# A spectral filter and a state-space recurrence on one core: units of 256 tokens by four state blocks, B kept in SBUF, and the inverse transform carried to the output tiles

## The chip, the cores and the metric

The kernel runs on one core of one Trainium2 chip. The metric is device time in microseconds (us), the median of several executions. The engines are called as in the profile: PE is TensorE's matmul, PEld its weight load, DVE is VectorE, ACT is ScalarE, POOL is GpSimd, and SP is SyncE, whose queue (SPq) issues nearly all DMAs here. L12 means line 12 of the kernel that was profiled.

## The reference, cut to what matters

```python
# x: [1, 2048, 1024]; all inputs bf16
g = sigmoid((x * gate_w).sum(-1, keepdims=True))
a = irfft2(rfft2(x) * (w_r + 1j * w_i))            # over tokens and channels
Lam_bar = exp(dt * Lam); B_bar = ((Lam_bar - 1) / Lam)[:, None] * Bmat
Bu = einsum("bld,pd->blp", x, B_bar)               # 1024 complex states
for t in range(2048): h = Lam_bar * h + Bu[:, t]   # kept for every t
b = 2 * einsum("blp,dp->bld", hseq, Cmat).real + x * Dskip
out = g * a + (1 - g) * b
```

The kernel does the two-dimensional FFT as matrix products in stages, with one transposition through DRAM on the way forward and one on the way back. The recurrence is done by rotating into a frame in which the state only shrinks by a real factor: two products by cosine and sine tables, a scan on VectorE, two products back. In both kernels FFT work and recurrence work are interleaved.

## The kernel before: what the change and the argument touch

B is loaded transposed in the first of four token chunks, stored to a DRAM scratch, and loaded again from it in the other three. A recurrence unit is 512 tokens by two state blocks.

```python
TC = 512
def fetch_BT(c, jb):
    BTs = btp.tile([P, 2, 8, P], BF16, name="BTs")               # two buffers
    if c == 0:
        for ri, src in enumerate((B_B_re, B_B_im)):
            nc.sync.dma_start_transpose(out=BTs[:, ri], in_=src[P * jb:P * (jb + 1), :])
        nc.sync.dma_start(out=bt_dram[jb], in_=BTs)
    else:
        nc.sync.dma_start(out=BTs, in_=bt_dram[jb])
    BTq[c, jb] = BTs

def ssm(c, q, u, h):
    sh = [P, 2, 2, TC]
    # two products by the table, add, subtract        ... (cut)
    for j in range(2):
        jb = 2 * q + j
        rb = r_sb[:, jb:jb + 1].to_broadcast([P, TC])
        for ri in range(2):
            nc.vector.tensor_tensor_scan(out=g[:, j, ri, :], data0=rb, data1=v[:, j, ri, :], ...)
    # two products by the table, add, subtract        ... (cut)
```

The two columns of W that need a correction (k = 0 and k = 512) are loaded:

```python
nc.gpsimd.dma_start(out=Wc[:, :, 0], in_=Wr_v[:, :, 0])          # and three more like it
```

The inverse FFT ends with two small products for each of 16 groups of tokens. The first is evicted to ZT; the second consumes it at once, and the result goes to a DRAM scratch that the last stage reads again:

```python
ZT = gt.tile([P, 8, P], BF16, name="ZT", tag="gev")
nc.scalar.copy(out=ZT, in_=psz.rearrange("p kc (c q) -> p (kc c) q", c=2))
...
nc.tensor.matmul(psy[:, cls, :], lhsT=ZT[:, 4 * cls + i, :], rhs=Gi_sb[:, 4 * cls + i, :], ...)
...
nc.sync.dma_start(out=ga_v[:, bp, :], in_=ga.rearrange("p h n -> p (h n)"))
```

The start loads four x tiles, then the first block of B (two transposing loads and the store), then the other x tiles as buffers come free:

```python
for r in range(4):
    load_x(r)
fetch_BT(0, 0)
for r in range(4):
    turn_x(r)
    load_x(r + 4)
```

## Time and profile before

| | before |
|---|---|
| time, median of 4 runs beside the changed kernel | 462.67 us (458.96 to 470.05) |
| span of the profiled run | 464.6 us (that run took 466.38 us, 1.6% above the fastest, so it is marked slow) |
| TensorE busy | 378.8 us |
| VectorE busy | 289.4 us |
| DMA | 67.30 MB |
| first B product | 63.5 us |
| first FFT matmul | 72.3 us |

A run is called slow when it lies more than 1.5% above the fastest run of the same kernel. The only trace of the kernel before is of a slow run, so its stage times are read with that in mind.

The page gives busy time for each engine, then the span in 40 slices of 11.6 us: a digit is the busy share in tenths, PEclk the granted TensorE clock in tenths.

```profile
PE 378.8 (82%) x1958; PEld 185.3 (40%) x1993; DVE 289.4 (62%) x420; ACT 191.8 (41%) x251; POOL 5.9 (1%) x11
...
PE   2005599899999675988895998899998999997996
...
PEclk9999689999999997999998899999999999999799
DMA  8999306464546999878867546431212223310121
```

TensorE is the busiest engine. The holes are the first five slices, the stretch from slice 14 to 20, and single slices later. The table of stretches (length, busy time and instruction count of each engine, clock, DMA share, GB/s) shows the first hole and part of the second:

```profile
0.00:20.00 20.00, 4.00 (x29) 2.89 (x29) 4.01 (x23) 6.22 (x10) 5.87 (x11) 1.00 0.88 144
20.00:40.00 20.00, 2.91 (x19) 2.04 (x20) 2.41 (x13) 2.09 (x3) 0.00 (x0) 1.00 1.19 172
40.00:63.00 23.00, 14.78 (x110) 7.79 (x109) 11.87 (x16) 19.86 (x30) 0.00 (x0) 0.78 0.45 150
...
145.00:180.00 35.00, 23.00 (x131) 9.89 (x132) 31.29 (x57) 11.86 (x15) 0.00 (x0) 0.95 0.99 255
```

In the first 63 us TensorE works 22 us. From 145 to 180 us VectorE (31.29 of 35 us) and the DMA engines (0.99) are nearly full and TensorE is not. The list of waits (waiting engine, line, releaser: total us, times, longest) names what held TensorE:

```profile
PE pt L165 <- DMA xn<-in_A_x_dram: 26.3, 3, 22.3
PE psu L276 <- DMA BTs<-bt_scratch: 14.0, 6, 5.5
```

So x came late at the start, with one wait of 22.3 us, and TensorE waited 14 us for reloads of B.

### The profile page before, as it was taken

To read this page: it belongs to the slowest core of one execution; us is meant where nothing else is said; L and a number is where in the kernel's file an instruction comes from. 1 tells how busy PE (TensorE), PEld (TensorE's weight loads), DVE (VectorE), ACT (ScalarE), POOL (GpSimd) and SP (SyncE) were. 2 spreads that over 40 slices of the span, in tenths; PEclk is the share of its full clock that TensorE was granted. 3 is DMA by queue.
4 is the path that set the end of the run, shared out by engine and by line. 5 is a ranking of instruction groups with operands and counts; after the bars stand their busy time and mean duration, and the time that the engine had idled before them with its cause. 6 is when DMAs were issued, how large, how long until landed. Compare 5 with 4: busy or idle time off the path is not lost.

```text
span 464.6 us, 5250 instructions
## 1 busy us (share of the span) xinstructions
PE 378.8 (82%) x1958; PEld 185.3 (40%) x1993; DVE 289.4 (62%) x420; ACT 191.8 (41%) x251; POOL 5.9 (1%) x11
## 2 busy tenths in 40 slices
PE   2005599899999675988895998899998999997996
PEld 1003235444444231433341555544444444443442
DVE  2012556667868899798993121259995269999212
ACT  0406989899965431366660566640000011110000
POOL 5000000000000000000000000000000000000000
PEclk9999689999999997999998899999999999999799
DMA  8999306464546999878867546431212223310121
GB/s 138 116 134 343 103 9 139 145 194 136 164 153 227 181 289 243 179 245 263 276 216 125 165 161 223 156 117 45 82 56 92 90 92 136 108 62 13 47 89 45
DMA packets 71153, 67.30 MB, mean 145 GB/s; under 512 B 45780, under 2 KB 50260, under 8 KB 70744
## 3 DMA queue, kind: packets, MB, share of 16 engines
q1 hardware_dynamic: 70280, 65.08, 49.9%
q10 hardware_dynamic: 656, 1.88, 2.1%
q0 software_dynamic: 192, 0.02, 0.8%
q8 instruction: 15, 0.25, 0.2%
q14 instruction: 10, 0.08, 0.1%
HBM read 37.57 MB, written 21.00 MB: 126 GB/s over the span
## 4 chain that ended last, share of the span: by engine, by line
PE 36%; DVE 14%; DMA 9%; issue 5%; ACT 4%; SPq 3%; ACTq 0%; DVEq 0%
PE ps_y L547 15%; PE psu L276 11%; DVE g L294 5%; PE ps_id L489 5%; DMA BTs<-bt_scratch 4%; DMA Bb<-turn_scratch 2%; ACT eo L492 2%; DVE o L556 2%; DVE pb L302 2%; PE ps_fd L326 1%; DMA W_b<-in_A_w_r_dram 1%; PE ps_y L551 1%; SPq L653 1%; DMA W_b<-in_A_w_i_dram 1%; DVE pa L301 1%
## 5 line engine op out<-in xcount | busy, mean ns | idle before, releaser
L276 PE MATMUL psu<-xT,BTs 128*128 128x512 bf16 x498 | 121.2, 384 | 15.1 <-DMA BTs<-bt_scratch 14.0
L547 PE MATMUL ps_y<-CT_1199,h 128*128 128x512 bf16 x250 | 96.2, 385 | 5.6 <-DVE o L556 5.1
L547 PE MATMUL ps_y<-CT_1200,h 128*128 128x512 bf16 x250 | 96.2, 385 | 0.3
L276 PEld LDWEIGHTS <-BTs 128*128 128x128 bf16 x512 | 49.5, 99 | 74.2 <-DMA BTs<-bt_scratch 17.7
L547 PEld LDWEIGHTS <-h 128*128 128x128 bf16 x512 | 49.6, 99 | 61.2 <-issue 8.3
L278 ACT CAST u<-psu 128x1024 bf16<-128x1024 f32 x32 | 32.3, 1014 | 84.7 <-PE psu L276 80.1
L294 DVE TENSOR_TENSOR_SCAN g<-r_sb,carry,v 128x512 bf16<-128x512 f32 x48 | 58.4, 1266 | 0.0
L556 DVE SCALAR_TENSOR_TENSOR o<-ps_y,omg,gac 128x1024 bf16<-128x1024 f32 x16 | 20.5, 1279 | 37.4 <-PE ps_y L551 37.4
L165 PE MATMUL pt<-ident,xn 128*128 128x128 bf16 x128 | 11.6, 254 | 31.9 <-DMA xn<-in_A_x_dram 26.3
L494 DVE TENSOR_TENSOR ga<-eo 128x512 bf16<-128x512 bf16 x16 | 6.8, 425 | 47.9 <-ACT eo L492 47.9
L326 PE MATMUL ps_fd<-G_sb,preT 128*128 128x512 bf16 x125 | 29.9, 379 | 3.9 <-ACT X_684 L329 1.0
L489 PE MATMUL ps_id<-Gi_sb,ZT 128*128 128x512 bf16 x126 | 29.9, 378 | 3.1 <-ACT eo L492 3.0
L285 DVE TENSOR_TENSOR v<-u,tab 128x2048 bf16<-128x2048 bf16 x16 | 19.6, 1223 | 16.0 <-ACT u L278 15.8
L492 ACT ACTIVATE eo<-ps_id,gA 128x1024 bf16<-128x1024 f32 x16 | 17.8, 1115 | 17.1 <-issue 14.6
L326 PEld LDWEIGHTS <-preT 128*128 128x128 bf16 x128 | 18.5, 144 | 15.3 <-issue 6.2
L166 ACT COPY xT<-pt 128x1024 bf16<-128x1024 bf16 x16 | 15.3, 1007 | 20.6 <-PE pt L165 20.6
L165 PEld LDWEIGHTS <-xn 128*128 128x128 bf16 x128 | 9.6, 115 | 35.2 <-DMA xn<-in_A_x_dram 28.1
L298 ACT CAST glast<-g 128x4 f32<-128x4 bf16 x12 | 2.4, 199 | 48.1 <-DVE g L294 48.1
L301 DVE TENSOR_TENSOR pa<-g,tab 128x2048 bf16<-128x2048 bf16 x16 | 19.6, 1224 | 0.4
L489 PEld LDWEIGHTS <-ZT 128*128 128x128 bf16 x128 | 12.4, 97 | 18.1 <-issue 5.6
L286 DVE TENSOR_TENSOR su<-u,tab 128x2048 bf16<-128x2048 bf16 x16 | 19.5, 1219 | 0.0
L302 DVE TENSOR_TENSOR pb<-g,tab 128x2048 bf16<-128x2048 bf16 x16 | 19.5, 1218 | 0.0
(553 smaller groups left out, 487.3 us busy)
## 6 DMA issues: line engine op xcount, KB each, us to landing
BTs<-bt_scratch SPq DMA_DIRECT2D x24, 512.0 KB, 4.4
xn<-in_A_x_dram SPq DMA_DIRECT2D x16, 256.0 KB, 3.7
bt_scratch<-BTs SPq DMA_DIRECT2D x8, 512.0 KB, 2.7
Bb<-turn_scratch SPq DMA_DIRECT2D x16, 256.0 KB, 4.1
Cq<-turn_scratch SPq DMA_DIRECT2D x16, 256.0 KB, 2.7
ga_scratch<-ga SPq DMA_DIRECT2D x16, 256.0 KB, 2.4
gac<-ga_scratch SPq DMA_DIRECT2D x16, 256.0 KB, 4.4
out_dram<-o SPq DMA_DIRECT2D x16, 256.0 KB, 2.1
```

The lines of the kernel that those rows point to most:

```text
L165: nc.tensor.transpose(out=pt[:, j8, :], in_=xns[r][:, P * j8:P * (j8 + 1)], identity=ident)
L276: nc.tensor.matmul(psu[:, ri, :], lhsT=BTs[:, ri, d8, :], rhs=xT[:, d8, TC * c:TC * (c + 1)], start=(d8 == 0), stop=(d8 == 7))
L278: nc.scalar.copy(out=u_out, in_=psu)
L285: nc.vector.tensor_mul(out=v, in0=u, in1=tab[:, js, 0:1, :].to_broadcast(sh))
L294: nc.vector.tensor_tensor_scan(out=g[:, j, ri, :], data0=rb, data1=v[:, j, ri, :], initial=(0.0 if c == 0 else carry[:, jb, ri:ri + 1]), o ...
L301: nc.vector.tensor_mul(out=pa, in0=g, in1=tab[:, js, 2:3, :].to_broadcast(sh))
L302: nc.vector.tensor_mul(out=pb, in0=g[:, :, ::-1, :], in1=tab[:, js, 3:4, :].to_broadcast(sh))
L326: nc.tensor.matmul(ps[:, cls, :], lhsT=preT_A[:, cls, d4, j, :], rhs=G_sb[:, cls, d4, :], start=(d4 == 0), stop=(d4 == 3))
L489: nc.tensor.matmul(psy[:, cls, :], lhsT=ZT[:, 4 * cls + i, :], rhs=Gi_sb[:, 4 * cls + i, :], start=(i == 0), stop=(i == 3))
L492: nc.scalar.activation(out=eo, in_=psy, func=ACT.Copy, scale=gA[:, bp:bp + 1])
L547: nc.tensor.matmul(psy[:, 512 * dh:512 * (dh + 1)], lhsT=hs[jb // 2][:, jb % 2, ri, P * tq:P * (tq + 1)], rhs=CT[ri][:, jb, 512 * dh:512 * ...
L556: nc.vector.scalar_tensor_tensor(out=o, in0=psy, scalar=omg[:, tb:tb + 1], in1=gac, op0=ALU.mult, op1=ALU.add)
```

## The change

Its intent: take the B scratch and the FFT result scratch away, run the forward FFT first and without interruption, halve the rotation tables, and do the last product of the inverse FFT beside the output product C of each token tile, so that the FFT result need not be stored in between.

```diff
-TC = 512
+TC = 256
+NEARLY = 4
...
+    BT = [btp.tile([P, 2, 8, P], BF16, name=f"BT{jb}") for jb in range(8)]      # B stays
+    xn = [t.rearrange("p r j m -> p r (j m)") for t in BT]                     # x is loaded there first
+    for i in range(8):
+        nc.sync.dma_start(out=xn[i], in_=x[2 * P * i:2 * P * (i + 1), :].rearrange("(r p) d -> p r d", p=P))
...
+    def unit(c, q):                                  # 256 tokens by four state blocks
+        u = b_unit(c, q)
+        ...  # same products and sums, in place; 8 scans of 256 in place of 4 of 512
...
             A1 = gta.tile([P, 2, K], BF16, name="A1")
-            nc.scalar.copy(out=A1, in_=psa)
-            nc.scalar.copy(out=Acol[:, j, :], in_=psa[:, :, 0])
+            nc.vector.tensor_copy(out=A1, in_=psa)
+            nc.gpsimd.tensor_copy(out=Acol[:, j, :], in_=A1[:, :, 0])
             nc.sync.dma_start(out=turn1_dram[j], in_=A1)
...
-            ZT = gt.tile([P, 8, P], BF16, name="ZT", tag="gev")
-            nc.scalar.copy(out=ZT, in_=psz.rearrange("p kc (c q) -> p (kc c) q", c=2))
+        ZT = fft["ZT"]                               # [P, 8, 16, P]: all 16 groups at once
+        ZT_v = ZT.rearrange("p i q (a b) -> p b i q a", b=16)
+        for bp in range(16):
+            ...
+            nc.scalar.copy(out=ZT_v[:, bp], in_=psz.rearrange("p kc (c q a) -> p (kc c) q a", c=2, a=8))
...
+    def finish(tb, psy=None):                        # for one tile of 128 tokens
+        pse = psU.tile([P, 2, K], FP32, name="ps_id", tag="psu")
+        ...  lhsT=fft["ZT"][:, 4 * cls + i, tb, :], rhs=fft["Gi"][:, 4 * cls + i, :]
+        ...  # scale by g, add and subtract, add (1 - g) times the C product, store to the output
...
-        nc.gpsimd.dma_start(out=Wc[:, :, 0], in_=Wr_v[:, :, 0])
-        ...  # three more
+            for ri, W in enumerate((A_w_r, A_w_i)):
+                fl = W.rearrange("s k -> (s k)")[K:K + (S - 1) * (K + 1)].rearrange("(s k) -> s k", k=K + 1)
+                nc.sync.dma_start(out=Wp[0:P - 1, ri], in_=fl[0:S - 16, 0:2].rearrange("(p b) k -> p b k", b=16))
+                ...  # three small loads for what is left
```

First, the final token order is 128 consecutive tokens to a tile, while group bp of the inverse FFT yields tokens bp, bp + 16, and so on; so the copy to ZT now writes 2-byte elements 32 bytes apart. The last element of one row of W lies next to the first of the following row, so both columns are now loaded as pairs, 4 bytes each.

## The prediction

> **What bounds the kernel now.** By the page, TensorE is busy 379 of 465 us. Its pitches in the timeline (start to start, full clock) are 0.216 us for 512 columns, 0.109 for 256; so all matmuls need 346 us, and about 118 us is lost. The table of stretches and the waits show where:
> - Start, 0 to 63 us: 22 us of TensorE work. The longest wait is 22.3 us for x tiles: in the timeline the DMA queue stands from 7 to 33 us at the store of B, behind two transposing loads; VectorE stands 17.75 us for W columns.
> - 145 to 256 us (forward product, W): TensorE 87 of 111 us, VectorE 96, DMA share 0.76 to 0.99; B reloads waited for 14 us. After a 5.0 us wait at 254.7, 256-column matmuls step 0.213 us for 4 us. The Trainium skill (TensorE: Matmul & The Clock Gate, Part 1) says that an idle window of about 3.4 us halves the clock; this trace agrees.
> - End: from 417 to 432 us VectorE's recurrence holds TensorE up.
>
> **What changes.** Removed: 4 MB of B stores, 12 MB of reloads, 8 MB of FFT result scratch, gate scratch, the column patch (8 us near 245). Halved: table making. Added: 4 MB of float32 scratch, 64 scans. A scan steps 1.18 us for 512 elements; I estimate 0.65 for 256, 5.2 us a unit against 4.7. A unit then costs VectorE 12.9 us (4 products at 1.16, 4 sums at 0.63, scans, carry). A1 (1.15 us, 16 times) and half the x evictions move from ScalarE to VectorE. B's 1024 matmuls of 256 columns take 112 us, as before.
>
> **Timeline of the new order.**
> - Start: x first in the queue; 4 MB at 90 ns per 2048-byte packet on 16 engines, 14 us. VectorE's evictions and sums, 22 us: forward FFT begins near 27.
> - Forward FFT, 16 steps: matmuls 1.9, ScalarE 1.31, two handovers: 3.4 us a step (5.1 before), to 82.
> - Turn through DRAM, filled with B products, 17 us and the fixup: to 100.
> - W stage, 16 steps: VectorE bounds it, 15 x 1.9 plus three units, 67 us; DMA about 3.6 us a step, close behind. To 169.
> - Then TensorE-bound: is2 14, inverse 28, B 62, C 118: 222 us, VectorE 176. ScalarE costs is2 4 to 6 us; gaps and cold clock 8; tail 5.
>
> Sum about 410: 36 us saved at the start, the rest mostly in the middle.
>
> **Prediction: 410 us, range 395 to 428. Chances: faster 0.97, same 0.02, slower 0.01.**
>
> **What would show it.** First FFT matmul at 24 to 32 us; forward steps 3.2 to 3.7 us apart; W stage 62 to 80 us, VectorE over 90% busy; 256-scans near 0.65 us pitch; B matmuls at 0.109; from the first C product on TensorE busy over 93%, no bubble in the last 40 us; DMA bytes near 46 MB.
>
> **What would make it wrong.** The transposing B loads (16 behind x in one queue, each waiting for TensorE to leave its buffer) could arrive late and delay the T3 table and the stores. The six shared h buffers could hold VectorE after the sixth unit (I expect 15 us, off the critical path); if VectorE cannot catch up, the C stage is VectorE-bound, +10 to 20. DMA latency with two buffers in the W stage: +10. In-place products or 256-element rows slower than 1.16: +5.

## The result

| | before | after |
|---|---|---|
| time, median of 4 runs | 462.67 us | 497.5 us (495.55 to 499.25) |
| ratio, 95% interval | 1 | 1.0781 (1.0698 to 1.0863): slower |
| span profiled | 464.6 us | 495.2 us |
| TensorE busy | 378.8 us | 391.8 us |
| VectorE busy | 289.4 us | 314.5 us |
| DMA | 67.30 MB | 46.37 MB |
| first B product | 63.5 us | 27.1 us |
| first FFT matmul | 72.3 us | 29.9 us |

A ratio here compares the fast runs of the two kernels in the same rounds, while the medians are taken over all runs, so it is not quite the ratio of the medians quoted beside it. The spread of the kernel before from run to run (459 to 470 us here) is wider than that of most variants.

The start came out as foreseen: the first B product came 36.4 us earlier. DMA fell by a third; yet the kernel lost 35 us. The page after, same lines (a slice is now 12.4 us):

```profile
PE 391.8 (79%) x2568; PEld 244.5 (49%) x2601; DVE 314.5 (64%) x532; ACT 211.6 (43%) x195; POOL 18.3 (4%) x42
...
PE   4797306989979777554444699999999999999994
...
PEclk9789656999989999965555599999999999999999
DMA  8999012213418998862210202200120130001001
```

There are two new holes. In slices 5 and 6 (3 and 0 tenths) TensorE nearly stops. In slices 18 to 23 it is "busy" about half the time at a granted clock of 5 to 6 tenths. From slice 24 to the end it is full, as predicted. The table of stretches of the kernel after:

```profile
46.00:78.00 32.00, 6.03 (x22) 2.92 (x21) 2.34 (x3) 4.41 (x8) 0.70 (x4) 0.61 0.17 33
...
146.00:212.00 66.00, 49.16 (x307) 29.11 (x311) 61.24 (x112) 36.51 (x52) 9.48 (x16) 0.99 0.89 228
212.00:281.00 69.00, 34.71 (x152) 21.50 (x152) 23.41 (x36) 66.13 (x17) 0.00 (x0) 0.52 0.22 68
...
342.00:444.00 102.00, 101.53 (x689) 66.16 (x697) 99.32 (x149) 22.53 (x22) 0.00 (x0) 1.00 0.14 47
```

The W stage (146 to 212) is bound by VectorE, 61.24 of 66 us, as predicted, and the stage of the C products has no bubble. From 212 to 281 us only ScalarE is full, 66.13 of 69 us, in 17 instructions, and the TensorE clock is 0.52. From 46 to 78 us no engine is busy for more than 6.03 of the 32 us.

**Stretch 212 to 281.** The instructions of the line that copies to ZT (duration min/median/max in ns, first and last start), and the chain that ended last (start, length, what):

```profile
L455 ACT CAST ZT<-ps_is_2045 x1: 4751/4751/4751, 241.5 to 241.5; 128x1024 bf16<-128x1024 f32 x1
L455 ACT CAST ZT<-ps_is_2057 x1: 4747/4747/4747, 245.8 to 245.8; 128x1024 bf16<-128x1024 f32 x1
```

```profile
211.47 4.24 DMA Cq<-turn_scratch
215.77 64.80 ACT ZT L455 x15
```

The copies of 128x1024 elements take 4.75 us each and start 4.3 us apart. A copy of the same shape and types, PSUM to bf16, takes 1.01 us elsewhere in the same trace, as this line of the page shows (busy us, mean ns of one):

```profile
L260 ACT CAST u<-psu 128x1024 bf16<-128x1024 f32 x32 | 32.2, 1012 | 60.9 <-PE psu L258 47.0
```

The same copy to ZT took 1.00 us in the kernel before, where it was contiguous. Fifteen of the slow copies are 64.80 us in a row on the chain. TensorE works about 2 us between two of them and then idles. The Trainium skill (TensorE: Matmul & The Clock Gate, Part 1) puts the half clock down to idle windows of about 3.4 us. This trace agrees only in part: the slow matmuls begin after a wait of 5.5 us (L258, for the eviction u), but the waits for the copies were only 2.0 to 2.8 us, and the mean clock of the stretch was 0.52 all the same. With contiguous copies (first experiment below) it was 0.99 in this stage, from 216 to 232 us.

**Stretch 46 to 78.** The SP queue in order of time (start, length of the issue on the queue, line, destination and source):

```profile
45.98 0.38 SPq L325 DMA_DIRECT2D turn_scratch<-A_602  x1
46.40 0.88 SPq L586 DMA_DIRECT2D Wp<-in_A_w_r_dram  x1
47.33 12.27 SPq L587 DMA_DIRECT2D Wp<-in_A_w_r_dram  x1
...
60.52 0.71 SPq L586 DMA_DIRECT2D Wp<-in_A_w_i_dram  x1
61.34 12.04 SPq L325 DMA_DIRECT2D turn_scratch<-A_622  x1
```

L586 is the load of 127 partitions, once for the real and once for the imaginary part. Its own issue takes 0.7 to 0.9 us; the next issue then stands for 12.27 and 12.04 us. The second time the one that stands is the store of an A1 tile of the forward FFT. TensorE meanwhile waits for VectorE to evict the next A1 tile:

```profile
L318 PE MATMUL ps_s_677<-X_655,T_sb 128*128 128x512 bf16 x1 | 0.6, 586 | 23.6 <-DVE A_662 L323 23.6
```

VectorE is held in two ways by the same queue. A1 has two buffers, and the standing store (issued at 61.34, landed 13.7 us later, at 75.0) holds one of them. And before this eviction VectorE has a small cast of the W columns (Wc_f) to do, for which it waited from 50 to 76.9 us, because GpSimd (which sorts the columns, Wc) waited for the column loads:

```profile
POOL Wc L592 <- DMA Wp<-in_A_w_i_dram: 33.0, 1, 33.0
DVE Wc_f L357 <- POOL Wc L593: 26.9, 1, 26.9
```

The cast ended last: the A1 tile was evicted right behind it, at 77.0 us. Which of the two would have cost how much alone was not tested.

The DMA view of this window, 46 to 75 us in 40 slices, shows what the engines did:

```profile
DMA  6961000000000000000000000000000000000054
GB/s 183 314 220 6 1 1 1 1 1 1 1 1 1 1 1 1 1 1 1 1 0 0 1 1 1 1 1 1 1 1 1 1 1 1 1 1 1 1 198 164
```

The share of 16 engines rounds to 0 and the rate is 1 GB/s: about one engine moves 4-byte pieces. The load has 127 x 16 = 2032 pieces, and 2032 pieces in 12 us are 5.9 ns each.

**A third line** stands high in the list of waits of the kernel after:

```profile
DVE h L288 <- DMA y_scratch<-ye: 64.9, 1, 64.9
```

VectorE waited 64.9 us for a buffer of h, where the prediction had foreseen 15 us and called it off the critical path. It might be a third cause, so it is tested too.

### The profile page after: what moved, and what is told of

It reads as the page before. It is cut to its first block, busy times and chain, and to the rows that moved or that the text cites. A ratio compares the mean times of both kernels' runs of the same rounds, so it can differ in the third digit from the quotient of the medians.

```text
span 495.2 us, 6444 instructions
## 1 busy us (share of the span) xinstructions
PE 391.8 (79%) x2568; PEld 244.5 (49%) x2601; DVE 314.5 (64%) x532; ACT 211.6 (43%) x195; POOL 18.3 (4%) x42
## 2 busy tenths in 40 slices
DMA packets 60991, 46.37 MB, mean 94 GB/s; under 512 B 42658, under 2 KB 47138, under 8 KB 60578
## 4 chain that ended last, share of the span: by engine, by line
PE 54%; ACT 21%; SPq 8%; DVE 6%; DMA 6%; issue 3%; POOL 1%; ACTq 0%; POOLq 0%; another core or an unknown queue 0%; DVEq 0%
PE ps_y L512 23%; PE psu L258 14%; ACT ZT L455 13%; PE ps_id L530 6%; PE ps_fd L306 4%; SPq L587 3%; SPq L325 3%; DMA Bb<-turn_scratch 2%; PE pt L551 2%; DVE u L277 2%; PE ps_y L516 1%; SPq L503 1%; DMA vec_97<-in_B_Dskip_dram 1%; DMA W_b<-in_A_w_r_dram 1%; DMA Cq<-turn_scratch 1%
## 5 line engine op out<-in xcount | busy, mean ns | idle before, releaser
L277 DVE TENSOR_TENSOR_SCAN u<-r_sb,carry,u 128x256 bf16<-128x256 f32 x112 | 74.6, 730 | 0.0
L288 DVE TENSOR_TENSOR h<-u,tab 128x2048 bf16<-128x2048 bf16 x16 | 19.5, 1217 | 64.9 <-DMA y_scratch<-ye 64.9
L533 ACT ACTIVATE eo<-ps_id,gB 128x1024 bf16<-128x1024 f32 x16 | 17.8, 1113 | 99.1 <-PE ps_id L530 99.1
L306 PE MATMUL ps_fd<-G_sb,preT 128*128 128x512 bf16 x125 | 31.9, 397 | 3.9 <-ACT X_813 L309 0.5
L530 PE MATMUL ps_id<-Gi_sb,ZT 128*128 128x512 bf16 x124 | 29.4, 379 | 0.2
L453 PEld LDWEIGHTS <-Cq 128*128 128x128 bf16 x64 | 8.8, 138 | 39.0 <-issue 35.9
L258 PE MATMUL psu<-xT,BT_118 128*128 128x256 bf16 x128 | 17.9, 288 | 5.5 <-ACT u L260 5.5
L270 DVE TENSOR_TENSOR u<-u,tab 128x2048 bf16<-128x2048 bf16 x16 | 19.6, 1223 | 0.4
L287 DVE TENSOR_TENSOR sg<-u,tab 128x2048 bf16<-128x2048 bf16 x16 | 19.5, 1218 | 0.1
L258 PE MATMUL psu<-xT,BT_114 128*128 128x256 bf16 x128 | 17.8, 283 | 0.1
L258 PE MATMUL psu<-xT,BT_119 128*128 128x256 bf16 x128 | 17.6, 280 | 0.0
L258 PEld LDWEIGHTS <-BT_118 128*128 128x128 bf16 x128 | 13.2, 103 | 8.7 <-issue 5.7
L258 PE MATMUL psu<-xT,BT_117 128*128 128x256 bf16 x128 | 17.5, 280 | 0.0
```

Source lines behind the costliest of these rows:

```text
L258: nc.tensor.matmul(psu[:, j, ri, :], lhsT=BT[jb][:, ri, d8, :], rhs=xT[:, d8, TC * c:TC * (c + 1)], start=(d8 == 0), stop=(d8 == 7))
L270: nc.vector.tensor_mul(out=u, in0=u, in1=bc(0))
L277: nc.vector.tensor_tensor_scan(out=u[:, j, ri, :], data0=rb, data1=u[:, j, ri, :], initial=(0.0 if c == 0 else carry[:, jb, ri:ri + 1]), o ...
L287: nc.vector.tensor_mul(out=sg, in0=u[:, :, ::-1, :], in1=bc(3))
L288: nc.vector.tensor_mul(out=h, in0=u, in1=bc(2))
L306: nc.tensor.matmul(ps[:, cls, :], lhsT=preT_A[:, cls, d4, j, :], rhs=G_sb[:, cls, d4, :], start=(d4 == 0), stop=(d4 == 3))
```

## The experiments

Three theories were open at first. A: the copies to ZT are slow because they write with a 32-byte step. B: the loads of the W columns to 127 partitions run on one DMA engine, come late themselves and stop the queue. C, the rival of A: the stage is stretched because VectorE waits for the h buffers (64.9 us), and the copies are merely there.

### ZT written contiguously, wrong result on purpose

```diff
-        ZT_v = ZT.rearrange("p i q (a b) -> p b i q a", b=16)
+        ZT_v = ZT
...
-            nc.scalar.copy(out=ZT_v[:, bp], in_=psz.rearrange("p kc (c q a) -> p (kc c) q a", c=2, a=8))
+            nc.scalar.copy(out=ZT_v[:, :, bp, :], in_=psz.rearrange("p kc (c m) -> p (kc c) m", c=2))
```

The tokens come out in the wrong order, and nothing else changes, not even the order of instructions.

> The changed kernel with ZT written in contiguous runs of 128 elements instead of steps of 32 bytes; the later reads are left as they were, so the result is wrong on purpose. Every engine's order is otherwise unchanged. Theory A (the 32-byte step of the write makes the 16 copies slow): the copies fall from 4.75 us to 1.0 to 1.3 us, the stage from the first copy to the first C product from 65 us to 18 to 24 us, TensorE keeps its full clock there, and the whole takes 497 - 45 = 446 to 458 us. Rival B (the stage waits for the Cq loads or for TensorE at half clock): the copies' length changes but the stage stays above 45 us. Rival C (VectorE, held 65 us by the shared h buffers, is what counts): the time stays within 2% of 497, because VectorE then has to catch up its 8 units later.

Measured: 446.26 us (445.85 to 448.24), ratio to before 0.9765 (0.9673 to 0.9857). The line of the copies:

```profile
L455 ACT CAST ZT<-ps_is x16: 1012/1012/1012, 216.1 to 232.0; 128x1024 bf16<-128x1024 f32 x16
```

All 16 copies take 1.012 us in place of 4.75, and the last starts at 232.0 us instead of 280.1. The wait of VectorE for h shrank from 64.9 to 13.1 us by itself: it was an effect of the copies. In the program ScalarE evicts the tiles ye, which share those buffers, after the copies, so it is likely that it came to them late; that link was only argued. From the first copy to the first C product the stage took 16 us in place of 65. Theory A holds; C falls, and so does the expectation's rival B, a stage above 45 us.

### The W column load split at 112 partitions

```diff
-  nc.sync.dma_start(out=Wp[0:P - 1, ri], in_=fl[0:S - 16, 0:2].rearrange("(p b) k -> p b k", b=16))
+  nc.sync.dma_start(out=Wp[0:112, ri], in_=fl[0:1792, 0:2].rearrange("(p b) k -> p b k", b=16))
+  nc.sync.dma_start(out=Wp[112:P - 1, ri], in_=fl[1792:S - 16, 0:2].rearrange("(p b) k -> p b k", b=16))
```

The Trainium skill (DMA: Bandwidth & Descriptors, "Why a DMA increments its semaphore by 16 and not by 1", the paragraph on how many engines) states that the number of engines is the largest one up to 16 that divides the size of the slowest dimension (of both sides of the transfer), and names 127 partitions as a case that gets one engine. By that rule 112 partitions get 16 engines and the other 15 get 15. The bytes and the pieces stay the same.

> The changed kernel with each load of W columns to 127 partitions cut in two, 112 and 15 partitions: same bytes, same 4-byte pieces, same queue, same order. Theory A (127 partitions put all 2032 pieces on one DMA engine, which takes 12 us, and the queue behind it stands still, twice): the two stalls of 12.3 and 12.0 us fall below 3 us each, the forward FFT loses its gap of about 24 us, and the whole takes 470 to 476 us. Rival B (some 4000 tiny pieces in this queue cost the time however they are spread): the stalls stay, 495 us. Rival C (the gap is TensorE waiting on VectorE or on T3): the stalls shrink, the gap stays.

Measured: 471.5 us (470.51 to 472.69), correct, ratio to before 1.0317 (1.0196 to 1.0438). The SP queue of this run:

```profile
45.62 0.74 SPq L586 DMA_DIRECT2D Wp<-in_A_w_r_dram  x1
46.41 0.98 SPq L587 DMA_DIRECT2D Wp<-in_A_w_r_dram  x1
47.44 1.72 SPq L588 DMA_DIRECT2D Wp<-in_A_w_r_dram  x1
...
50.15 0.36 SPq L325 DMA_DIRECT2D turn_scratch<-A  x1
```

No issue stands for 12 us any more; the longest of the column loads is 1.72, and VectorE waits 1.3 us for the columns in place of 26.9. The forward FFT ends 26 us earlier, and the copies to ZT still take 4.745 us. Theory B holds, independently of A, and what the traces show agrees with the rule of the skill in both cases, 127 and 112; which engines carried the pieces was not looked at.

### ZT written in runs of four, correct result

Four groups are gathered in one PSUM tile, and the copy writes four neighbouring elements (8 bytes) at a time, still at a 32-byte step, reading PSUM with a stride instead.

```diff
-        for bp in range(16):
-            ...
-            nc.scalar.copy(out=ZT_v[:, bp], in_=psz.rearrange("p kc (c q a) -> p (kc c) q a", c=2, a=8))
+        G = 4
+        for b0 in range(0, 16, G):
+            ...  # four Cq tiles; for each kc the products of the four groups side by side in psz
+                nc.scalar.copy(out=ZT_g[:, 256 * k0:256 * (k0 + 4 // G), b0:b0 + G].rearrange("p (k m) b -> p k m b", m=256),
+                               in_=psz.rearrange("p k b m -> p k m b"))
```

> A correct version: four of the 16 column sets are gathered in one PSUM tile, so that a copy writes runs of 4 neighbours (8 bytes) at the 32-byte step, with a strided read of PSUM. If the cost goes with the number of separate 32-byte steps written (1024 a copy before, 256 now): copies of 1.2 to 1.7 us, whole 450 to 462 us. If it goes with elements whose neighbours in time lie apart, or if the strided PSUM read is slow: copies stay above 3 us, whole above 480 us.

Measured: 448.19 us (446.79 to 449.9), correct, ratio 0.98 (0.9704 to 0.9896). The line of the copies in the trace:

```profile
L461 ACT CAST ZT<-ps_is x16: 1012/1012/1059, 218.9 to 241.9; 128x1024 bf16<-128x1024 f32 x16
```

The same elements land at the same places, four at a time, at full speed. So it is not the 32-byte step between runs that costs, but a run of only one element at such a step; and the strided read of PSUM cost ScalarE nothing in this copy.

### Both repairs

> Both repairs together: W columns loaded to 112 and 15 partitions, and ZT written in runs of 4 by column sets gathered in groups of four. The gaps lie in different stages, so if nothing else hides behind them the gains add: 497.5 - 49 - 26 = 422 us (416 to 430), ratio to the kernel before 0.90 to 0.93. If VectorE becomes the limit once both gaps are gone (it has to finish the last unit before TensorE can finish): above 435 us, with TensorE idle in the last third.

Measured with five rounds: 424.86 us (421.48 to 425.84), correct; before in the same rounds 461.28 us; ratio 0.9238 (0.9173 to 0.9303). The page of this run:

```profile
PE 376.9 (89%) x2568; PEld 238.6 (56%) x2601; DVE 314.6 (74%) x532; ACT 157.8 (37%) x195; POOL 15.8 (4%) x42
...
PE   4699599899798678939999999999999999999994
...
PEclk9869889999989998977999999999999999999998
```

Both holes are gone, and the time lies inside the predicted range. One slice of 3 tenths is left, the 18th, between the W stage and the first copies to ZT. The two gains add up: by the ratios to before, the copies in runs of four are worth 1.0781 - 0.98 = 0.098 and the split load 1.0781 - 1.0317 = 0.046, together 0.144; both at once gave 1.0781 - 0.9238 = 0.154.

### How the cost depends on the step: 16 bytes and 8 bytes, wrong results on purpose

```diff
-  ZT_v = ZT.rearrange("p i q (a b) -> p b i q a", b=16)
+  ZT_v = ZT.rearrange("p i q (c a b) -> p c b i q a", a=8, b=8)      # b=4 in the second run
...
-  nc.scalar.copy(out=ZT_v[:, bp], in_=...)
+  nc.scalar.copy(out=ZT_v[:, bp // 8, bp % 8], in_=...)              # 4 in the second run
```

> The changed kernel with the copies to ZT stepping 16 bytes instead of 32 (wrong result on purpose, order unchanged). The Trainium skill (SBUF - State Buffer) speaks of 16-byte lines and of two hits needed on each: by that a 16-byte step should cost as much as a 32-byte one, 4.75 us a copy. If it is the distance that counts: about 2.5 us.

> The same with a step of 8 bytes (two elements to a 16-byte line): by the skill's rule at full speed, 1.0 to 1.3 us a copy; by a cost that grows with the distance about 1.5 to 2 us.

The line of the copies in the trace, with the step of 16 bytes:

```profile
L455 ACT CAST ZT<-ps_is x16: 4672/5001/5030, 215.6 to 283.0; 128x1024 bf16<-128x1024 f32 x16
```

The same line with the step of 8 bytes:

```profile
L455 ACT CAST ZT<-ps_is x16: 2400/2503/2529, 217.6 to 251.2; 128x1024 bf16<-128x1024 f32 x16
```

The whole kernels took 500.31 and 467.22 us, one run each (state unknown). The Trainium skill (SBUF — State Buffer, Specifications, the row on cachelines; also Advanced Engine Details and Errata, SBUF Cachelines) states 16-byte lines and that at least two hits on a line are needed for full bandwidth. The runs agree that a step of a line or more is slow (5.00 us at 16 bytes, 4.75 at 32). They disagree if the rule is read, as the expectation read it, to say that two hits are enough: at an 8-byte step two elements fall in each line, and the copy still took 2.50 us, about 2.5 times the 1.01 us of the contiguous one. The measurement decides. Four neighbouring elements were enough; two neighbours were not tried.

The kernel has one more copy of this shape with a step, that to X1 in the forward FFT: it writes every second element, 4 bytes apart (trace of both repairs):

```profile
L309 ACT CAST X<-ps_fd x16: 1275/1304/1317, 32.8 to 90.7; 128x1024 bf16<-128x1024 f32 x16
```

So the durations are 1.01 us contiguous, 1.30 at 4 bytes, 2.50 at 8, 5.00 at 16, and no more at 32. From 8 to 16 bytes the cost doubles with the number of lines entered (512 and 1024, 4.9 ns a line: an estimate, 2.50 us / 512 and 5.00 us / 1024). But the copy to X1 and the one in runs of four both enter 256 lines, and they took 1.30 and 1.01 us; so a count of lines alone is not the rule, and none is shown.

### Every second copy by VectorE

```diff
-  nc.scalar.copy(out=ZT_v[:, bp], in_=...)
+  (nc.vector.tensor_copy if bp % 2 else nc.scalar.copy)(out=ZT_v[:, bp], in_=...)
```

> The changed kernel with every second copy to ZT on VectorE, same 32-byte step, correct result. If the step is dear on both engines: VectorE's copies also take 4 to 5 us, the two work side by side, the stage falls from 65 to about 35 us, the whole to about 468 us. If only ScalarE pays: VectorE's copies take about 1.2 us and the stage about 40 us.

Measured in one look: 481.93 us (one run, state unknown), correct. The line of the copies, now on two engines:

```profile
L455 ACT CAST ZT<-ps_is x8: 4463/4530/4719, 218.3 to 264.7; 128x1024 bf16<-128x1024 f32 x8
L455 DVE CAST ZT<-ps_is x8: 4454/4494/4716, 220.1 to 267.9; 128x1024 bf16<-128x1024 f32 x8
```

VectorE's contiguous copies of this shape, to A1, are on the page of the same run:

```profile
L323 DVE CAST A<-ps_s 128x1024 bf16<-128x1024 f32 x16 | 19.5, 1219 | 15.8 <-PE ps_s L321 10.8
```

VectorE pays nearly the same for such a write, 4.49 us against its own 1.22; the cost goes with the pattern written and is not ScalarE's alone. The expectation for the time was missed by some 14 us: the copies did not simply run side by side. Within this stage, which took 54 us (218 to 272) where half of the 69 us before would have been 34, ScalarE waited 13.7 us and VectorE 5.5 us for TensorE, and TensorE 18.3 us for the copies, at a mean clock of 0.69. Why the two engines did not overlap further was not followed up.

### Are the h buffers or the Cq loads the next limit?

Both are edits of the kernel with both repairs: seven h buffers for six, and eight Cq buffers (the loads that feed this stage) for six.

```diff
-    hp = ctx.enter_context(tc.tile_pool(name="hp", bufs=6, side="left"))
+    hp = ctx.enter_context(tc.tile_pool(name="hp", bufs=7, side="left"))
```

> The kernel with both repairs and seven instead of six buffers for h, ye and yl. VectorE waits 22.7 us for a buffer there. If that wait lies off the critical path (TensorE is busy 97% from then on): within 1% of 425 us although the wait shortens. If it feeds the end: 405 to 415 us.

Measured: 423.48 us (422.24 to 424.81), ratio 0.933 (0.9269 to 0.9392). The wait for h fell from 22.7 to 17.4 us, but the time by 1.4 us at most: by the medians, less than the spread; by the ratio (0.9238 before this edit) not at all. So the wait is off the critical path as far as these 5.3 us can show, and as the prediction had it.

```diff
-        fft["cq"] = dctx.enter_context(tc.tile_pool(name="cq", bufs=6, side="left", reuse_waits="tile"))
+        fft["cq"] = dctx.enter_context(tc.tile_pool(name="cq", bufs=8, side="left", reuse_waits="tile"))
```

> The kernel with both repairs and eight instead of six buffers for Cq, so that two whole groups of four loads fit. The chain shows three waits of about 2.7 us for Cq between groups: if they are load latency that a second group in flight hides, the stage falls by 5 to 8 us and the whole to 417 to 420 us; if they wait for the last stores of the column scratch or for ScalarE: unchanged.

Measured: 421.52 us (420.11 to 422.93), ratio 0.929 (0.9212 to 0.9368). The waits for Cq went, and the last copy to ZT starts at 207.9 us instead of 217.6; but the medians differ by only 3.3 us, in different batches, and the ratio did not fall (0.9238 before this edit). So little or nothing of what the stage gave back was time saved. By its median this is the fastest version measured, but it is not clearly apart from the one with both repairs.

### Was the reading of the old start right?

The prediction said that in the kernel before x stood behind the store of B. Here each store of B is issued one load later, in the kernel before:

```diff
-            nc.sync.dma_start(out=bt_dram[jb], in_=BTs)
+            if jb:
+                nc.sync.dma_start(out=bt_dram[jb - 1], in_=BTprev[0])
+            BTprev[0] = BTs
```

> The kernel before with one thing moved: each store of B to its scratch is issued one load later, so that three further x loads no longer stand behind it. My reading of the start (x loads stand from 7 to 33 us behind the store of B, which waits for two transposing loads): the first B product moves from 63.5 us to 48 to 56 us and the whole falls by 6 to 14 us. Rival (the transposing loads and the 1.5 MB table fill the DMA engines in that time, and x would come no sooner wherever the store stands; VectorE waits for W columns as well): under 4 us.

Measured: 463.21 us (462.04 to 465.24), correct. The kernel before had a median of 463.38 in these rounds, but four of its seven runs were slow; against its three fast ones (453.41 to 454.38) this run is 2% longer, ratio 1.021 (1.0143 to 1.0277). Either way there is no gain. First the SP queue of the kernel before, then that of this run:

```profile
6.52 0.60 SPq L578 DMA_DIRECT2D G_sb<-c_G  x1
32.66 0.32 SPq L266 DMA_DIRECT2D bt_scratch<-BTs  x1
33.08 1.20 SPq L160 DMA_DIRECT2D xn<-in_A_x_dram  x2
```

```profile
6.45 0.63 SPq L583 DMA_DIRECT2D G_sb<-c_G  x1
7.13 11.67 SPq L266 DMA_TRANSPOSE BTs<-in_B_B_re_dram  x1
18.92 8.22 SPq L160 DMA_DIRECT2D xn<-in_A_x_dram  x2
```

The first B product came 4.7 us earlier (58.8 for 63.5 us, the latter in a slow run), and TensorE's longest wait for x was 16.6 us. With the store out of the way, the transposing load stood 11.67 us and the x loads 8.22 us in its place. So that one store is not what held the old start. The expectation's rival, that the DMA engines were full with other transfers, fits: the DMA list of the kernel before gives 28.5 us for the 1 MB table G to land and 27.0 us for the 1.5 MB table T. It was not tested, and what holds the first 30 us is left open.

### Does the store of A1 explain the rest?

After both repairs the forward FFT still takes longer than predicted. Both kernels start from the version with eight Cq buffers. In the first, the first three stores of A1 go out by ScalarE's queue; in the second, the last eight loads of B stand later in the program.

```diff
-            nc.sync.dma_start(out=turn1_dram[j], in_=A1)
+            (nc.scalar if j < 3 else nc.sync).dma_start(out=turn1_dram[j], in_=A1)
```

> With both repairs in place (and eight Cq buffers) 421.5 us was measured against 410 predicted, and the forward FFT stage still takes 65 us against 55. In the run with both repairs the first A1 tile, ready at 36.4 us, was issued to DRAM only at 46.3, behind the transposing loads of B; VectorE then stood 6.0 us for its buffer and TensorE 3.9 us for VectorE. Here the first three stores of A1 go out by ScalarE's queue. Theory (the stores stand behind the B loads, and that is on the path): the 6.0 and 3.9 us waits go, the stage shortens by 4 to 5 us, total about 417 us. Rival (the stage is held by the making of the tables on ScalarE and VectorE between the steps, and the store only fills that time): the waits shift to other instructions, total 420 to 423 us.

Measured: 431.16 us (424.8 to 433.26), correct, two runs fast (424.8 and 429.23) and two slow; ratio 0.9354 (0.9119 to 0.959). The fast runs lie 0.8% and 1.8% above 421.52 us, and the interval overlaps that of the version it started from (0.9212 to 0.9368): it is no gain, against the theory, and whether it is a loss is not shown. The waits of ScalarE from 30 to 60 us show a new cost:

```profile
ACT X L309 <- DMA BT<-in_B_B_re_dram: 4.6, 1, 4.6
ACT ang L228 <- DMA Wp<-in_A_w_r_dram: 4.0, 1, 4.0
```

In the timeline ScalarE issues the first two stores at the end of these waits (at 44.09 and 49.74 us), so it stood with them, 4.6 and 4.0 us, for a transposing load and a W column load that neither the stores nor its own next instructions read. Why the stores waited for these loads the trace does not show. TensorE's wait for A1 is down to 0.3 us, but later in this run ScalarE stood 10.8 us more for the first Cq load, so the run says little about the question asked.

```diff
-    for jb in range(2, 8):
+    for jb in range(2, 4):
         load_B(jb)
...
     pull(15.0)
+    for jb in range(4, 8):
+        load_B(jb)
```

> The same kernel as the run with eight Cq buffers, with the loads of the last four state blocks of B later in the program: in the queue one store of A1 then stands one pair of transposing loads earlier, and the small tables stand before the last eight. Theory (stores behind B loads): the first store goes out about 3 us earlier, at 43 us instead of 46, so the waits of 6.0 and 3.9 us shrink to about 3 and 1 us: 418 to 420 us. Rival (tables): 420 to 423 us.

Measured: 422.27 us (421.7 to 424.43), correct, ratio 0.9266 (0.9177 to 0.9356). The first store went out at 41.8 us instead of 45.7, and VectorE still stood 6.8 us for A1 buffers (6.6 before); the second store left at 49.6 (50.5 before). The time did not move, which is what the rival said; but as the waits did not shrink either, the theory was not truly tested.

## Why the prediction was wrong

| stage | predicted | after | both repairs |
|---|---|---|---|
| start, to the first FFT matmul | 27 us | 29.9 | 29.4 |
| forward FFT, 16 steps | 55 | 89 | 65 |
| turn through DRAM and fixup | 18 | 25 | 25 |
| W stage, to ScalarE's next eviction of u | 69 | 67 | 67.5 |
| ZT stage, inverse, B and C, to the end | 240 | 284 | 237 |
| sum | 409 | 495 | 424 |

The boundaries are read from first and last starts in the traces; predicted numbers are those of the prediction, with its gaps, clock and tail put in the last row.

Right, with what was measured:

- The first FFT matmul came at 29.9 us (24 to 32 was given), and the first B product 36.4 us earlier (36 was given as the gain at the start).
- The steady step of the forward FFT was 3.33 us (3.4 predicted): six steps from 71.63 to 91.61 us in the run with both repairs.
- The W stage was bound by VectorE at 93% and took 67 us.
- The scans of 256 step 0.655 us (0.65), the 256-column matmuls 0.109 us, a unit costs VectorE 13.0 us (12.9), DMA bytes are 46.37 MB (46).
- The C stage ran without a bubble, and the wait for h buffers, larger than foreseen, was indeed off the critical path.

Wrong, by step:

1. **"ScalarE costs is2 4 to 6 us."** This term was mis-sized. I took the copy's duration from other copies of the same shape, without looking at its output pattern, although the diff shows the rearrangement that puts 32 bytes between elements. The trace before even held a hint: the copy to X1, also rearranged, took 1.30 us against 1.00 for the contiguous copy to ZT. The copy took 4.75 us instead of 1.01, 16 times. From the first copy to the first C product it was 65 us, where the prediction's 14 us for is2 and these 4 to 6 make about 19. Taking the step away gave 51 us by the medians and 47 by the ratios (0.102 of 462.67). The mechanism, ScalarE on the path in this stage, was as written. The slow copies also brought TensorE's clock down (0.52 in the stretch, 0.99 without them) and produced the long wait for h.
2. **No term for the W column loads.** "Removed" and "Added" count bytes, and these loads are 8 KB each. The two loads to 127 partitions held the queue for 12.27 and 12.04 us, the A1 stores stood behind them, and VectorE, which needs the columns before the next A1 tile, stood 26.9 us. The split load gave 26 us by the medians and 21 by the ratios (0.046 of 462.67). The prediction had named a queue that delays the stores as a risk, but had put it down to the transposing B loads.
3. **"The DMA queue stands at the store of B."** As the cause of the old start this falls with the deferred store, which gained nothing. The size of the gain was nonetheless right (36.4 us), in part by luck: the change removed the whole arrangement, not that store alone.
4. **The forward FFT and the turn**, after both repairs, are still 10 and 7 us over. In the trace of both repairs the first five steps are the long ones: the evictions of A1 start at 35.19, 40.86, 49.55, 52.79 and 57.41 us. The tables are being made then, and the stores stand behind the B loads. Two attempts to tell these apart failed, and the turn was not tested, so these steps of the prediction failed for a cause that stays open: the last 15 us are located and not explained.

With terms 1 and 2 repaired the kernel takes 424.86 us, within the range of 395 to 428, though still 15 us above the point. The large idea of the change was sound; two lines of bookkeeping in it cost 73 us (497.5 - 424.86).

## What to carry to other kernels

When a copy's output is rearranged, cost it from a copy with the same innermost step in bytes, not from one of the same shape; and if the order of the data must change, let each write keep a few neighbouring elements together (four were enough here). For a DMA, ask how many engines its outer dimension lets it use and how many pieces it has, before counting its bytes, and look at what stands behind it in the same queue and at who waits for it. A new wait that is long, as the 64.9 us here, need not be a cause: see whether it leaves by itself when the suspected cause is taken away.

## What the Trainium skill lacked or had wrong

- SBUF — State Buffer, and Advanced Engine Details and Errata (SBUF Cachelines): no number is given for the penalty. For a 128x1024 eviction from PSUM to bf16 by ScalarE these runs show 1.01 us contiguous, 1.30 at a step of 4 bytes, 2.50 at 8, 5.00 at 16 and 4.75 at 32; VectorE took 1.22 contiguous and 4.49 at 32.
- The same pages ask for at least two hits on a line for full bandwidth. Two were not enough here: two elements to a line at an 8-byte step took 2.50 us and not 1.01; runs of four neighbouring elements at a 32-byte step took 1.01.
- DMA: Bandwidth & Descriptors: the traces agree with the rule on the number of engines for 127 and 112 partitions. The section cited does not give what follows in the queue: a load of 2032 pieces of 4 bytes, at 1 GB/s, held the next issue for 12.27 us and 12.04 us, although those DMAs were another transfer and, the second time, a plain 256 KB store.
- TensorE: Matmul & The Clock Gate: with waits of only 2.0 to 2.8 us, repeated every 4.3 us, behind one of 5.5 us, the mean granted clock over 69 us was 0.52. The passage cited speaks of idle windows of about 3.4 us; elsewhere the page says that frequent short idles can make the clock swing, but gives no length for them.
